# One pair of token tiles goes from a full to a seven-product second layer, in a fused windowed attention and squared-ReLU layer kernel, with a new order of all engines

## The chip, the cores and the metric

The kernel runs on one core of a Trainium2 chip. The metric is device time in microseconds (us) of one execution, lower is better. The profile is of one execution; its "span" runs from the first to the last instruction of the program.

## What is computed

Attention with a sliding window of 128 and 4 sink keys over 4 batches, 8 heads, 768 positions and 64 channels; its output, heads side by side, is the input of two matrix products with a squared ReLU between them. Inputs and output are float32; the kernel computes in bfloat16 and accumulates in float32.

```python
scores = scale * q @ k.T                      # per batch and head
keep = (key < 4) | ((0 <= row - key) & (row - key < 128))
a = softmax(where(keep, scores, -1e9))
x = (a @ v).transpose(0, 2, 1, 3).reshape(3072, 512)
r = maximum(x @ w_in, 0.0)                    # w_in 512 x 2048
out = (r * r) @ w_out                         # w_out 2048 x 512
```

## The kernel before

**Tiles.** A batch has six token tiles of 128 rows, taken as three pairs, (b, 0) to (b, 2). Attention of a pair: scores on TensorE (`ps`, L540), exp on ScalarE (`expm`, L561), masks on VectorE or by two affine selects on GpSimd (L200), the sinks' share and the values on TensorE (`po`, L596 and L621), division on VectorE (`xn_sb`, L636 and L637), and a transpose to `xT`. Layer 1 (`pm`) writes the squares into `gT_sb`, 16 blocks of the hidden width by 768 tokens, one batch at a time. Layer 2 reads `gT_sb` and writes the output.

**The start.** q and k of batch 0 come by eight transfers on the queues of SyncE and ScalarE (`qr`, L316), are cast by any of three engines (`qs`), turned by TensorE against an identity matrix (`ident`, built by one affine select of GpSimd, L227) into a PSUM bank `pt`, and copied out to `qkT`. Everything else that is loaded goes through GpSimd's queue with a cast to bfloat16: values (L343), `w_in` (L283), q and k of later batches (L332) and `w_out` (L289). Each of these loads takes one of eight semaphores in turn, so a load waits until the load eight places ahead of it has landed.

**Layer 2, two ways.** `layer2` (L927) is the plain product: for both tiles of a pair 16 products each, 128 rows by 512 columns, 32 products in all, then two copies out of PSUM and a store. `layer2_fast` (L1037) is a Strassen-like scheme on the 2 x 2 blocks of (tile, half of the hidden width): seven products of half the columns, each in 8 matmuls of 256 columns, so 56 matmuls. Around them stand four sums of `gT_sb` blocks on VectorE (`sg`, L995, the second of which overwrites a block of `gT_sb`), two copies, two pair sums (L1062), a last quarter (L1078), a middle part (L1088) and a first quarter. It also needs four sums of halves of `w_out` (`wt`, L968, VectorE), which wait for all four `w_out` loads. `CLASSIC` lists the pairs that take the plain way.

**The order.** The kernel lists its steps as numbered operations with their needs; the string `ORDER` says in which order they are written, and on which engine each runs: `65g` is step 65 on GpSimd (p TensorE, v VectorE, a ScalarE, g GpSimd, s SyncE). Each engine works through its own steps strictly in that order, and a PSUM or SBUF buffer goes to the next step that takes one. `+n` puts n dummy matmuls ahead of a TensorE step (L174; L1222 for the first ones), which fill time in which TensorE would stand idle. At the `sinks` steps a `+1` means something else: it picks the form with 64 rows of the array in place of 128.

```python
o, e = self.ops[int(n[:-1])], {"p": "pe", "v": "dve", "a": "act", "g": "pool", "s": "sp"}[n[-1]]
self.dummies = int(dummies or 0)
o.run(e)
```

Of the kernel before, what the change touches and what calls it, by code (L numbers as in the profile page):

```python
# [15 lines left out]
ALU = mybir.AluOpType  # L16

ORDER = """
0v 5g 1v 9a 11a 2v 8s 10s 12s 13a 15a 55a 3g 896p+37 19g 20g 21g 22g 23g 56v 57p 58a 65a 66v 67p+20 59v 68a 79p 99p
69v 80p 101a 14s 61v 60g 62p 82a 71v 70g 72p+8 73a 64v 87p+2 74v 88p 81a 63v 108p 89a 90a 83p 85p 6g 76v 110a 91p  # L20
93p+6 77p 86v 24g 4g 25g 26g 84v 95p 16s 109p 18s 7s 75g 102g 121g 94v 27g 92v 97p+5 98v 28g 29g 30g 78a 96a 100p
105p+1 152p 31g 32g 33g 34g 111v 112a 113v 103a 114p 104v 115p 116v 153a 154a 106p 107v 158p 159v 117p 119p 35g 120a
36g 164p 118v 155p 156v 157a 165v 161p 162a 173p 17s 122p 124a 174v 125p 127a 123v 37g 38g 126a 167p 39g 40g 175a
204v 168v 163v 131p 134a 140p 143a 170p 41g 135g 128p 129a 130p 132a 133g 42g 139p 171v 289p 166v 290p 169v 136p 291p
292p 137p 144v 172a 293p 141a 145p 142v 146p 138v 294p 295p 147v 148p 150p 160v 296p 151v 149a 179p 43g 44g 45g 274v
176p 275v 297v 180a 298a 46g 200p 202v 192p 188p 177a 194v 201p 193p 195v 203a 189p 191v 47g 190a 196p 276v 197p 199v
215p 216a 178v 198a 205v 48g 185p 218a 186v 234p 182p 49g 50g 51g 52g 206p 235a 53g 54g 355g 356g 219v 373s 357g 277v
358g 237a 238g 226p 207a 229a 299s 227a 181v 278p 279p 280p 208p 281p 183v 184v 209a 249p 211a 246p 247a 236v 282p
248v 359g 254p 251v 187a 374s 250v 252p 210v 283p 257a 300v 301v 253a 255a 256g 360g 376s 284p 302v 262p 265a 239p+1
240p 217v 303v 285p 375s 361g 241v 377s 212v 304p 220p 221v 263a 286a 287a 305p 307p 306v 308p 396p 397a 399a 230v  # L30
228g 231p+1 232p 362g 378s 363g 364g 365g 366g 379s 311p 309v 213p 233v 242p 244p 310v 214v 367g 312p 243a 245a 222p
380s 368g 313v 314v 258g 385g 381s 382s 224p 225a 369g 223a 315p 316v 370g 383s 389p 390a 392a 322p 398v 331p 323a
384s 371g 372g 400v 401p 391v 324a 317a 402v 596g 318s 332v 597g 259p 260p 393v 266g 264v 319p 320a 325p 321a 326a
394p 261v 395v 334p 335a 413p 598g 616s 615s 414a 415g 416a 267p+1 268p 599g 328p 386v 327v 333v 270p 271a 269v 336a
626v 617s 329a 330v 272p 337p 614s 338a 339v 273a 340p 341a 417g 600g 601g 342v 441v 460v 405p 406a 408a 343p 404s
344v 443v 352p 403s 409g 464p 288s 353a 407g 423p 424a 425g 387p 388a 461v 602g 465p 603g 604g 605g 467p 469a 619s
354v 462v 618s 620s 466a 442v 349p 468p 426a 470v 350a 427v 431p 432a 434a 463v 498v 410p+1 433g 345a 411p 412v 471p
472p 630p 633a 631a 621s 418p+1 419p 473v 475p 351a 500v 474v 476v 632v 428p 429p 420v 430v 346p 445p 499v 501v 503a
504v 446p 436p 448p 507v 435g 444v 437p 477a 347a 348v 447a 438v 451v 522p 523p 449p 524a 525v 526p 440s 506v 505v
452p 450a 478s 453p 527v 454v 528p 646p 647a 529p 479v 480v 649a 455v 456p 457v 483p 484p 458v 627v 481v 654p 502v  # L40
485a 657a 486p 487p 508p 509p 488a 655a 634v 635p 489v 482v 656g 490p 510a 530a 421s 439s 422s 536v 512p 636v 606g
607g 511v 532p 533p 514p 513v 515p 516a 491p 537v 582p 538v 518p 492v 493v 534v 535a 584v 494p 495v 496a 497s 608g
622s 519p 520v 609g 610g 568p 570a 583p 569p 540p 517a 542a 586p 572p 554p 571v 585v 555p 587v 573v 588p 589p 556a
557v 539v 521a 574p 575p 558p 560p 559v 611g 459s 541p 531a 625s 682v 543v 544p 545v 561p 576a 648g 578p 579p 580v
650g 590a 562a 563a 624s 546p 547p 548a 683v 564p 565p 566v 577a 592p 593p 594v 550p 551p 658g 686p 552v 549a 637p
638a 612g 687p 640a 684v 639v 641v 623s 628p 629a 689p 664p 595a 659p+1 660p 688v 567v 690p 613g 665a 642p 685v 553v
667a 668g 666g 691a 693p 692v 694p 643v 661v 591a 695v 581a 720v 696v 721v 722v 723v 672p 675a 676v 651p+1 652p 653v
697p 724p 726a 725p 727p 644s 730v 673a 674v 645s 728p 731p 677p 678p 739a 740v 698v 729a 662s 663s 699a 700s 669p
679v 701v 670p 744p 745p 746a 671v 681s 743v 742v 732p 705p 758p 747v 702v 759p 735p 748p 760a 706p 708p 707a 680s
749v 741v 761v 762p 764p 703v 704v 750p 751p 763v 733v 752a 773v 734v 736v 711v 710v 774v 772v 709p 712p 737a 714v  # L50
715v 754p 765p 766a 767a 755p 756v 713p 775v 804p 806a 805p 807v 768p 769p 770v 716p 790p 791p 717v 792a 718a 753a
808p 809v 776p 777p 778v 793v 771v 818p 819p 820a 757a 821v 810p 822p 794p 811p 780p 824p 823v 825p 812a 826a 779v
782p 781v 814p 783p 828p 738s 784a 796p 832v 795v 797p 798a 834v 835v 833v 813a 829p 830v 815p 816v 786p 787p 800p
801p 802v 831a 788v 836p 837p 839p 841v 719s 838a 840p 842v 799a 843p 827v 803a 817a 844p 785v 847p 789a 845v 870v
874p 851v 852v 855p 856p 871v 858p 875p 846v 848v 872v 849a 850s 857a 873v 853v 854v 860v 877p 876a 859p 861v 862p
864v 865v 863p 866p 867v 868v 869s 878p 880v 881p 882p 879v 883v 884g 887v 885p 890s 889a 888v 892a 886p 891s 893s
894v 895a
"""


# [47 lines left out]
def kernel(  # L108
# [188 lines left out]


    NATURAL, TURNED, BIASED, FAST = (2, 3), (), 1, (2, 3)
    CLASSIC = ((0, 0), (0, 1))  # L300
    GROUPS = {b: [(0, 6)] for b in range(B)}
    GROUPS[0] = [(0, 4), (512, 2)]
    if 1 not in NATURAL:
# [877 lines left out]
    for b in range(B):  # L1181
# [29 lines left out]
        for u in range(NS):  # L1211
            if (b, u) in CLASSIC:
                layer2(b, u, by_part=True)
# [46 lines left out]
```

## Time and profile before

| | |
|---|---|
| three timed runs | 207.95, 208.26 and 208.32 us, median 208.26 |
| the profiled execution | 207.93 us, of which the span is 206.2 us |
| TensorE matmul | busy 200.5 us, 97% of the span, granted clock 0.999 |
| VectorE, ScalarE, GpSimd | busy 172.3, 127.7 and 102.8 us |
| transfers | 26.09 MB, of which 12.59 MB through GpSimd's queue |

In the profile's rows PE is TensorE's matmul stream and PEld its weight loads, DVE is VectorE, ACT ScalarE, POOL GpSimd, SP SyncE; a q behind the name means the engine's sequencer, which issues transfers. A row of the timeline has start, length, engine, source line, operation, output<-inputs, shapes, and how many instructions were merged. In the chain of waits a row has start, length and what the span's end hung on at that time. Matmuls overlap, so a matmul's own length (273 ns for 256 columns) is not its pace: the pace is the distance of starts, which the pieces of the chain give.

### The profile page before, as it was taken

Reading aid. Unit: us, or ns where it says so; the run is one execution under the profiler, and the core shown is the slowest. Engines: PE = TensorE matmul, PEld = TensorE weight load, DVE = VectorE, ACT = ScalarE, POOL = GpSimd, SP = SyncE. Lnnn points to the kernel's source line nnn. Section 1 sums busy time; section 2 is a strip of 40 time slices with the busy share of each in tenths; the row PEclk is TensorE's granted clock in tenths of the full one; section 3 lists DMA queues with packets and bytes.
Section 4 is the critical chain, followed back from the end, with each engine's and each line's share of the span. In section 5 each row is a group of like instructions: output and inputs, shape, how many; then the busy total and the mean of one; then the engine's idle time right before and its main releaser. Section 6 shows DMA issues by size and latency. Waiting matters only on the chain.

```text
span 206.2 us, 5651 instructions
## 1 busy us (share of the span) xinstructions
PE 200.5 (97%) x2362; PEld 168.5 (82%) x2366; DVE 172.3 (84%) x307; ACT 127.7 (62%) x167; POOL 102.8 (50%) x141
## 2 busy tenths in 40 slices
PE   7999999999999999999999999999999999999993
PEld 7659996588557856668889889998889999998983
DVE  5688478778969767969989998999898799999953
ACT  3696188138787585797794364798964146787100
POOL 7899866898908999767960009920220000000001
PEclk9999999999999999999999999999999999999999
DMA  5999999999996999999993448999024311200205
GB/s 192 278 188 206 170 202 214 165 153 149 137 208 53 109 110 172 168 182 137 109 173 78 139 69 52 210 191 63 3 52 120 88 55 50 106 0 0 105 0 203
DMA packets 93881, 26.09 MB, mean 126 GB/s; under 512 B 86816, under 2 KB 91552, under 8 KB 93856
## 3 DMA queue, kind: packets, MB, share of 16 engines
q0 software_dynamic: 69248, 12.59, 86.0%
q1 hardware_dynamic: 23232, 11.90, 26.0%
q10 hardware_dynamic: 1376, 1.25, 1.8%
q8 instruction: 18, 0.29, 0.6%
q14 instruction: 7, 0.06, 0.1%
HBM read 27.30 MB, written 6.29 MB: 163 GB/s over the span
## 4 chain that ended last, share of the span: by engine, by line
PE 85%; ACT 6%; DVE 4%; issue 2%; POOLq 0%; ACTq 0%; DVEq 0%
PE py L1037 25%; PE pm L838 18%; PE pm L698 17%; PE py L927 7%; PE po L621 5%; PE ps L540 4%; ACT expm L561 3%; PE warm L1222 2%; PE pt L438 2%; ACT r L709 1%; PE po L596 1%; PE px L666 1%; PE pt L428 1%; DVE sg L995 1%; PE pt L174 1%
## 5 line engine op out<-in xcount | busy, mean ns | idle before, releaser
L200 POOL TENSOR_SCALAR_AFFINE_SELECT expm<-expm 128x512 bf16<-128x512 bf16 x42 | 31.3, 782 | 41.3 <-ACT expm L561 41.1
L561 ACT ACTIVATE expm<-ps 128x1024 bf16<-128x1024 f32 (+1 forms) x48 | 43.7, 954 | 9.4 <-PE ps L540 8.7
L698 PE MATMUL pm<-xT,w_in_sb 128*128 128x256 bf16 (+1 forms) x320 | 44.5, 294 | 0.2 <-ACT expm L561 0.2
L698 PEld LDWEIGHTS <-w_in_sb 128*128 128x128 bf16 x320 | 34.3, 114 | 6.8 <-issue 0.9
L1037 PEld LDWEIGHTS <-gT_sb 128*128 128x128 bf16 x336 | 30.7, 98 | 4.2 <-issue 0.5
L1078 POOL TENSOR_TENSOR osb<-osb,u 128x256 f32<-128x256 f32 x1 | 0.7, 727 | 51.1 <-DVE u L1062 51.1
L1037 PEld LDWEIGHTS <-sg 128*128 128x128 bf16 x240 | 23.0, 98 | 2.7
L838 PE MATMUL pm<-xs,w_in_sb 128*128 128x128 bf16 (+1 forms) x256 | 23.4, 246 | 0.0
L838 PEld LDWEIGHTS <-w_in_sb 128*128 128x128 bf16 x256 | 21.9, 114 | 0.2 <-issue 0.2
L343 POOL DMA_DIRECT2D v<-in_v_dram x24 | 21.5, 905 | 0.1
L1037 PE MATMUL py<-wt,gT_sb 128*128 128x256 bf16 x160 | 20.8, 273 | 0.2 <-DVE gT_sb L995 0.2
L1037 PE MATMUL py<-wt,sg 128*128 128x256 bf16 x160 | 20.6, 273 | 0.0
L860 ACT ACTIVATE gT_sb<-r 128x1024 bf16<-128x1024 bf16 x19 | 19.4, 1053 | 1.5 <-DVE r L906 1.5
L709 ACT ACTIVATE r<-pm 128x1024 bf16<-128x1024 f32 x14 | 14.2, 1022 | 8.9 <-PE pm L698 8.9
L332 POOL DMA_DIRECT2D qn<-in_k_dram x20 | 17.8, 899 | 2.1 <-DMA v<-in_v_dram 1.0
L1037 PE MATMUL py<-w_out_sb,gT_sb 128*128 128x256 bf16 x144 | 18.7, 273 | 0.0
L332 POOL DMA_DIRECT2D qn<-in_q_dram x20 | 17.7, 894 | 1.8 <-DMA w_out_sb<-in_moe_w_out_dram 1.4
L879 DVE TENSOR_TENSOR t<-t,pm 128x512 f32<-128x512 f32 x24 | 16.0, 682 | 2.5 <-PE pm L838 2.0
L637 DVE TENSOR_TENSOR xn_sb<-po,rc 128x512 bf16<-128x512 f32 (+1 forms) x26 | 16.9, 650 | 0.9
L894 ACT ACTIVATE r<-pm 128x1024 bf16<-128x1024 f32 x12 | 12.1, 1020 | 8.8 <-PE pm L838 8.7
L838 PEld LDWEIGHTS <-qkT 128*128 128x128 bf16 x192 | 16.6, 114 | 0.1
L711 DVE TENSOR_SCALAR r<-pm 128x1024 bf16<-128x1024 f32 x10 | 12.1, 1220 | 4.6 <-PE pm L698 4.5
(99 smaller groups left out, 348.4 us busy)
## 6 DMA issues: line engine op xcount, KB each, us to landing
out_dram<-osb SPq DMA_DIRECT2D x11, 512.0 KB, 3.5
v<-in_v_dram POOLq DMA_DIRECT2D x24, 128.0 KB, 6.8
qn<-in_k_dram POOLq DMA_DIRECT2D x20, 128.0 KB, 6.5
qn<-in_q_dram POOLq DMA_DIRECT2D x20, 128.0 KB, 6.5
w_in_sb<-in_moe_w_in_dram POOLq DMA_DIRECT2D x4, 512.0 KB, 9.0
w_out_sb<-in_moe_w_out_dram POOLq DMA_DIRECT2D x4, 512.0 KB, 11.0
qr<-in_q_dram ACTq DMA_DIRECT2D x4, 256.0 KB, 6.6
qr<-in_k_dram SPq DMA_DIRECT2D x4, 256.0 KB, 6.2
```

The costliest lines, as they stand in the source:

```text
L200: nc.gpsimd.affine_select(out=e_tile, in_=e_tile, compare_op=ALU.is_ge, fill=fill, base=i - 1, pattern=[[0, n], [1 if i else -1, 128]], ch ...
L332: nc.gpsimd.dma_start(out=qn_t[b, ti][:, t, :].rearrange("p (h d) -> p h d", d=D), in_=(q, k)[ti][b, :, 128 * t:128 * t + 128, :].rearrang ...
L343: nc.gpsimd.dma_start(out=v_sb[b % 2][:, t, :, 0:D], in_=v[b, :, 128 * t:128 * t + 128, :].rearrange("h p d -> p h d"))
L561: nc.scalar.activation(out=x[:, :, o:512], in_=bank_t["s", b, s, m][:, :, o:512], func=AF.Exp, scale=scale)
L637: touch(("po", b, s, m0), e, nc.vector.tensor_tensor(out=xn_sb[:, 2 * s:2 * s + 2, :].rearrange("p i (j q h d) -> q p j i h d", j=2, q=2, ...
L698: nc.tensor.matmul(pm[:, i, :], lhsT=w_in_sb[:, fb // 4, kb, fb % 4:512:4], rhs=xT[:, c0 // 256:(c0 + cw) // 256, kb, :], start=(kb == 0), ...
L709: nc.scalar.activation(out=o, in_=h, func=AF.Relu)
L838: touch(tag, e, nc.tensor.matmul(y[:, bk, i, :], lhsT=weights(name, f0 + i, a), rhs=rhs[:, a, :], start=fresh and i == 0 and a == 0, stop= ...
L860: nc.scalar.activation(out=d, in_=x, func=AF.Square)
L879: touch(tag, e, nc.vector.tensor_tensor(out=T["t"], in0=T["t"], in1=T["y"][:, bk], op=ALU.subtract), bk)
L927: touch((b, u), e, nc.tensor.matmul(pm[:, i, :], lhsT=gT_sb[:, fb, 128 * t:128 * t + 128], rhs=w_out_sb[:, fb, :], start=(fb == 0), stop=( ...
L1037: ins = nc.tensor.matmul(y_, lhsT=x[:, i, :], rhs=r_, start=(first or tail and n == 2) and i == 0, stop=i == HB - 1, skip_group_check=not ...
```

## The change

Pair (0, 0), the first two token tiles of batch 0, leaves `CLASSIC`: its second layer is written by `layer2_fast`. Pair (0, 1) keeps the plain way, and all other pairs have the fast one already. Steps 278 to 288 become 278 to 296, and all later numbers rise by 8. The whole `ORDER` is another one, with another choice of engine at many steps and other counts of dummies; the rest of the program is the same.

```diff
-0v 5g 1v 9a 11a 2v 8s 10s 12s 13a 15a 55a 3g 896p+37 19g 20g 21g 22g 23g 56v 57p 58a 65a 66v 67p+20 59v 68a 79p 99p
+9a 11a 0v 1v 5g 8s 10s 12s 14s 13a 4g 15a 904p+43 19g 20g 3g 65g 21g 55v 56v 57p 58v 59a 60a 99p+13 101a 22g 66v 67p
...
-    CLASSIC = ((0, 0), (0, 1))
+    CLASSIC = ((0, 1),)
```

Counted over the order strings: the dummies are 37 + 20 + 8 + 2 + 6 + 5 before and 43 + 13 + 11 + 3 + 6 + 2 after, 78 both times. The sinks steps in the 64-row form are 8 of 16 before and 9 after; one more of them stands ahead of the first layer-1 step. VectorE has 7 in place of 10 relu steps of layer 1 and second-half quads, ScalarE 29 in place of 26; masks on GpSimd are 23 in place of 21.

Three places of the order matter below. The first is GpSimd at the start of the program, before the change, from the bias table of the scores (`biases`) on:

```order
L200 AFFINE_SELECT biases<-biases 128x2x128 x2
L237 COPY biases<-biases 128x512
L238 MEMSET biases 4x256
L227 AFFINE_SELECT ident<-ident 128x128
L343 DMA v_181<-in_v_dram 128x8x64 x2
L283 DMA w_in_sb<-in_moe_w_in_dram 128x4x512
L343 DMA v_181<-in_v_dram 128x8x64 x2
L184 CAST qs<-qr 128x512 x2
```

And the same place now:

```order
L200 AFFINE_SELECT biases<-biases 128x2x128 x2
L237 COPY biases<-biases 128x512
L238 MEMSET biases 4x256
L200 AFFINE_SELECT tri<-tri 128x128 x2
L343 DMA v_181<-in_v_dram 128x8x64 x2
L227 AFFINE_SELECT ident<-ident 128x128
L184 CAST qs<-qr 128x512
L283 DMA w_in_sb<-in_moe_w_in_dram 128x4x512
L343 DMA v_181<-in_v_dram 128x8x64 x2
L283 DMA w_in_sb<-in_moe_w_in_dram 128x4x512
L184 CAST qs<-qr 128x512
```

The identity matrix has moved behind the mask triangles (`tri`) and two loads of values, and the second cast behind two `w_in` loads.

The second is GpSimd in the middle, where it goes from loads for batches 1 and 2 to the masks of batch 1 (`expm`). Before:

```order
L343 DMA v_182<-in_v_dram 128x8x64 x2
L332 DMA qn<-in_k_dram 128x8x64 x2
L332 DMA qn<-in_q_dram 128x8x64 x2
L200 AFFINE_SELECT expm<-expm 128x4x128 x2
L343 DMA v_181<-in_v_dram 128x8x64
L200 AFFINE_SELECT expm<-expm 128x4x128 x2
```

And now, where `mask_168` is the mask table that batches from 1 on need for their first pair, which GpSimd built at 16 us before:

```order
L343 DMA v_182<-in_v_dram 128x8x64 x2
L332 DMA qn<-in_k_dram 128x8x64 x2
L332 DMA qn<-in_q_dram 128x8x64 x2
L343 DMA v_181<-in_v_dram 128x8x64 x2
L241 COPY mask_168<-tri 128x128
L242 COPY mask_168<-tri 128x256
L243 MEMSET mask_168 4x256
L200 AFFINE_SELECT expm<-expm 128x4x128 x8
```

Two loads of values and the table now stand ahead of four masks (two selects each) in one block.

The third is SyncE's queue at the end, with the stores of the last pair, before:

```order
L1120 DMA out_dram<-osb 128x1024
L1120 DMA out_dram<-osb 128x2x512
L1127 DMA out_dram<-osb 128x256 x2
L1135 DMA out_dram<-osb 128x128
L1255 UNCONDITIONAL_BRANCH
```

And now:

```order
L1120 DMA out_dram<-osb 128x1024
L1120 DMA out_dram<-osb 128x2x512
L1131 DMA out_dram<-osb 128x256
L1127 DMA out_dram<-osb 128x256
L1135 DMA out_dram<-osb 128x128 x2
L1255 UNCONDITIONAL_BRANCH
```

SyncE has four stores of the last pair in place of three, both halves of the last quarter (L1135) among them; ScalarE's queue has one in place of two.

More of the change, by code (lines that the diff above doesn't have):

```diff
@@ L18 @@
 ORDER = """
-0v 5g 1v 9a 11a 2v 8s 10s 12s 13a 15a 55a 3g 896p+37 19g 20g 21g 22g 23g 56v 57p 58a 65a 66v 67p+20 59v 68a 79p 99p
[L20 to L57, printed above, removed]
+9a 11a 0v 1v 5g 8s 10s 12s 14s 13a 4g 15a 904p+43 19g 20g 3g 65g 21g 55v 56v 57p 58v 59a 60a 99p+13 101a 22g 66v 67p
+61v 69v 62p+11 63a 23g 24g 64a 70g 71v 79p 81a 102v 16s 80p 68v 72p+3 73v 87p 74a 88p 83p 25g 26g 82a 76v 84v 108p 85p
@@ new lines @@
+89a 91p 90a 86v 93p+6 110a 77p 78a 109p 95p 92v 94v 97p+2 100p 7s 6g 75g 112a 111g 105p+1 114p+1 96v 98v 152p 113v
+115p 27g 28g 29g 30g 31g 103a 104v 106p 158p 116v 107v 117p 119p 32g 33g 34g 153a 154v 164p 118v 165v 159a 35g 36g
+120a 155p 156a 161p 162a 2v 204g 173p 122p 123a 125p 127v 126v 163a 124a 174v 167p 168v 37g 38g 139p 166a 141a 131p
+134a 39g 40g 41g 135g 42g 170p 43g 128p 129a 44g 45g 46g 47g 48g 49g 50g 51g 52g 53g 130p 157v 142v 132a 133v 54g 363g
+364g 140p 143a 365g 366g 297p 298p 144v 136p 145p 137p 138v 146p 147v 175a 169a 274v 275v 276v 277v 160a 171a 172a
@@ new lines @@
+299p 300p 278v 301p 302p 381s 279v 280v 148p 149a 367g 368g 303p 150p 151a 304p 305a 306a 307s 179p 180a 176p 177a
+200p 202v 192p 194a 193p 195v 201p 196p 203v 197p 199a 198v 178v 121g 188p 189p 190a 215p 185p 191v 205v 218a 216a
+234p 235a 237a 236g 238g 186v 281v 182p 206p 207a 181v 183a 226p 187v 282p 284v 283p 285p 184v 308v 383s 227a 208p
+288v 229a 211a 230g 228g 287v 369g 246p 209a 370g 371g 372g 373g 310v 384s 309v 286p 289p 249p 251a 247a 250a 210v
+291v 290p 248v 293p 374g 375g 376g 377g 219v 252p 254p 253a 292v 294v 382s 295v 255a 257a 217v 312p 314a 313p 212v
@@ new lines @@
+258g 262p 263a 256g 265a 231p+1 311v 315p 318v 232p 233v 213p 214v 316p 220p 266g 385s 319p 404p 221v 317v 388s 407a
+405a 239p+1 240p 241v 320p 222p 224p 225a 223a 242p 244p 243v 321v 245v 323p 397p 386s 398a 322v 324v 325a 342p 264g
+406v 400a 401v 333p 334a 17s 339p 343v 387s 390s 378g 379g 380g 408v 604g 18s 392s 340a 259p 260p 261v 389s 391s 399v
+330p 605g 623s 409p 410v 402p 403v 606g 607g 344v 331a 345p 346a 421p 422a 423g 424a 267p+1 335v 268p 341v 634v 348p
+336p 394v 347a 349a 350a 270p 269v 272p 332v 326s 271v 273v 425g 327p 328a 337v 338a 329v 622s 468v 469v 470v 625s
@@ new lines @@
+360p 413p 416a 361v 449v 471v 393g 351p 624s 352a 472p 473p 431p 608g 609g 450v 414a 415v 434a 432a 395p 475p 396a
+477v 474v 478v 451v 357p 358a 417g 476p 610g 611g 635v 612g 411s 412s 439p 506v 442a 418p+1 440a 419p 420v 479p 480p
+433v 638p 362a 296s 639a 641a 627s 613g 508v 626s 629s 481v 628s 353v 482v 426p+1 427p 428v 483p 435g 484v 485a 486s
+436p 453p 454p 430s 456p 437p 507v 438v 511a 512v 354p 640v 443g 359v 444p 452v 441g 445p 530p 531p 455a 457p 460p
+458a 532a 534p 446v 448s 459v 533v 429s 642v 513v 447s 355a 356a 462v 514v 461p 536p 654p 657a 655a 535v 464p 487v
@@ new lines @@
+537p 463v 488v 491p 492p 515v 465v 466a 467s 538a 662p 509v 489v 540p 490v 510v 493a 494p 663a 664g 665a 643p 495p
+614g 615g 644v 497v 544v 616g 617g 618g 539a 496a 516p 518a 517p 541p 546v 520p 519v 542v 498p 499p 656g 619g 547v
+576p 578a 521v 577p 522p 523p 590p 502p 620g 621g 579v 500v 501v 545v 524a 525a 526p 527p 580p 592a 591p 582p 594p
+631s 503v 504a 528v 543a 562p 564a 563p 581v 583p 630s 566p 548p 529a 593v 596p 595v 597p 658g 632s 565v 567v 690v
+666g 505s 691v 584a 550a 568p 569p 570a 549p 552p 586p 692v 587p 551v 553v 572p 588v 598a 554p 573p 585a 574v 555p
@@ new lines @@
+599a 556a 600p 601p 602v 694p 558p 559p 560v 561v 557a 645p 646a 696a 647v 648a 695p 649v 693v 633s 636p 637a 697p
+672p 675a 676g 571v 603v 700v 667p+1 668p 669v 698p 673a 650p 701p 651v 699a 703v 702p 674g 653s 652s 575a 589a 728v
+729v 680p 681a 730v 731v 659p+1 660p 704v 705p 706v 732p 683a 734a 682v 747a 707a 733p 735p 737a 684g 709v 749v 748v
+661v 670s 708s 736p 677p 678p 679v 739p 752p 753p 754a 755v 685p 710v 686p 766p 738v 756p 767p 768a 770p 687v 740p
+689s 743p 713p 769v 688s 771v 750v 714p 757v 758p 759p 760a 751v 741v 742v 744v 745a 711v 712v 716p 718a 715a 772p
@@ new lines @@
+773p 774a 775a 762p 763p 717p 671s 780v 720p 781v 719v 784p 785p 761a 764v 786a 787v 776p 777p 778v 765a 722v 723v
+721p 724p 788p 782v 789v 812p 814a 725v 726a 798p 800a 813p 816p 815v 817v 799p 826p 828a 779a 827p 818p 802p 819p
+820a 821a 801v 804p 829v 803v 840v 830p 832p 805p 790p 791p 783v 822p 823p 841v 806a 842v 808p 831v 833p 792a 794p
+824v 809p 810v 844p 845p 843v 746s 795p 796v 727s 834a 793a 836p 837p 838v 807a 847p 835a 849v 846a 848p 825a 850v
+851p 797a 852p 855p 811v 839a 859v 853v 863p 860v 854v 865a 861v 878v 864p 866p 856v 857a 862v 880v 867p 870p 868a
@@ L58 @@
+858s 879v 882p 883p 872v 869v 873v 871p 884v 888v 874p 875v 876a 885p 887a 886p 881v 889p 877s 891v 892v 897s 890p
+893p 894p 895v 896v 898a 899s 900v 901s 902a 903s
 """
```

## The prediction

> **What bounds the kernel now.** I read the busy shares first, then the slices, the chain that ended last, and last the chain's pieces in order of time.
>
> ```profile
> PE 200.5 (97%) x2362; PEld 168.5 (82%) x2366; DVE 172.3 (84%) x307; ACT 127.7 (62%) x167; POOL 102.8 (50%) x141
> PE   7999999999999999999999999999999999999993
> PE 85%; ACT 6%; DVE 4%; issue 2%; POOLq 0%; ACTq 0%; DVEq 0%
> 16.15 1.91 PE pm L698 x16
> ```
>
> TensorE is busy 97% of the span, and only its first and last slices are below 9 tenths. 85% of the chain is TensorE. The last row is the first piece of layer 1, at 16.15 us: from there TensorE has work without a hole until its last product, so the time is the **start** (16.15), the **sum of TensorE's pieces**, and the **tail** behind its last product. VectorE, at 84%, is the nearest rival.
>
> **Times.** The sum is made against the profiled execution, 207.93 us (span 206.2 and 1.7 around it). The median of the three runs is 208.26, 0.33 above it. I work out a difference and apply it to the median.
>
> **The products.** A piece gives the pace: its length over its count.
>
> ```profile
> 36.33 1.73 PE py L927 x8
> 65.74 2.62 PE py L1037 x24
> 18.06 0.23 PE po L596 x4
> 62.94 0.11 PE po L596 x4
> ```
>
> A full product takes 1.73 / 8 = 0.216 us, a half one 2.62 / 24 = 0.109. Pair (0, 0) had 32 full ones, 32 x 0.216 = 6.91 us; it gets 56 half ones, 56 x 0.109 = 6.11: **-0.80 us**. The third row is a sinks step in the 128-row form behind the first layer-1 step, the fourth one in the 64-row form. One such 0.23 step leaves the stream and stands now ahead of layer 1, where TensorE waits for others: **-0.23**. The dummies (78) and the number of changes between 64 and 128 rows behind the first layer-1 step (I count 40 in both orders) stay.
>
> **VectorE under it.** The fast pair adds four sums, two copies, two pair sums, two middle parts and two quarters; the plain copies go.
>
> ```profile
> 193.81 0.69 DVE L995 TENSOR_TENSOR sg<-gT_sb,sg 128x1024 bf16<-128x1024 bf16 x1
> 201.21 0.42 DVE L1062 TENSOR_TENSOR u<-py,u 128x256 f32<-128x256 f32 x1
> 40.00:50.00 10.00, 9.95 (x106) 8.31 (x104) 7.75 (x14) 5.31 (x9) 9.05 (x12) 1.00 2.68 152
> 50.00:60.00 10.00, 9.95 (x102) 6.23 (x103) 8.51 (x15) 7.62 (x11) 6.23 (x7) 1.00 2.44 163
> L711 DVE TENSOR_SCALAR r<-pm 128x1024 bf16<-128x1024 f32 x10 | 12.1, 1220 | 4.6 <-PE pm L698 4.5
> ```
>
> Four sums at 0.69 and some six small steps at 0.42 are 2.8 + 2.5 = 5.3 us. The windows (after the length: PE, PEld, DVE, ACT, POOL) show VectorE 7.75 and 8.51 busy of 10 where this lies, so 3.7 us are free there, and the three relus that leave VectorE (1.22 each, last row) free 3.7 more. I cost it at nothing, hidden by TensorE's stream; with the cover gone it would be 5.3 - 3.7 = 1.6 us. What is late next then are the masks and squares that VectorE makes for the same stretch.
>
> **The start.** GpSimd now makes the identity matrix behind the triangles and two loads.
>
> ```profile
> 3.33 0.28 POOL L227 TENSOR_SCALAR_AFFINE_SELECT ident<-ident 128x128 bf16<-128x128 bf16 x1
> 3.57 1.96 POOL L343 DMA_DIRECT2D v<-in_v_dram  x2
> 5.00 0.41 PE L428 MATMUL pt<-ident,qs 64*128 64x64 bf16 x16
> 5.47 0.60 ACT L181 ACTIVATE qkT<-pt 128x512 bf16<-128x512 bf16 x1 [0.53 <-PE pt L428]
> 8.72 0.58 PE L428 MATMUL pt<-ident,qs 64*128 64x64 bf16 x16
> 9.83 0.57 PE L428 MATMUL pt<-ident,qs 64*128 64x64 bf16 x16
> 10.96 3.13 ACT L561 ACTIVATE expm<-ps 128x768 bf16<-128x768 f32 x4
> 11.08 0.55 POOL L200 TENSOR_SCALAR_AFFINE_SELECT tri<-tri 128x128 bf16<-128x128 bf16 x2
> 15.05 1.94 ACT L561 ACTIVATE expm<-ps 128x1024 bf16<-128x1024 f32 x2
> 16.15 1.04 PE L698 MATMUL pm<-xT,w_in_sb 128*128 128x256 bf16 x8 [0.17 <-ACT expm L561]
> ```
>
> The identity was ready at 3.61. Now: 3.37 (end of the bias table) + 0.55 + 1.96 + 0.28, **6.1 to 6.2**, so the first transposes go from 5.00 to about 6.1. Behind them I went on by hand with the new order and these durations: copies out of the bank at 6.6, the casts that follow them, second transposes at 7.8, third at 8.9 (8.72 before: they wait for late q anyway), fourth at about 10.95 (9.83 before), and the exps begin at 11.9 instead of 10.96. A copy of 0.60 that ScalarE made between its exps (`xT`) is VectorE's now, so the exp that frees the bank for the last step ahead of layer 1 ends at 16.3, not 16.1. Behind it still stands a sinks step of 0.11 with its change of rows, so layer 1 begins at about 16.55: **+0.40**. The ends: +1.1, if the whole delay of the identity passes through, and -0.6, if nothing of it does and the copy's 0.60 is won. The value lies by the row it is nearest to, that of the exps.
>
> **The tail.**
>
> ```profile
> 201.67 0.80 DVE L1094 TENSOR_TENSOR osb<-py,u 128x256 f32<-128x256 f32 x2
> 201.84 1.06 PE L1037 MATMUL ya<-w_out_sb,gT_sb 128*128 128x128 bf16 x16
> 202.12 0.82 SPq L1127 DMA_DIRECT2D out_dram<-osb  x2
> 202.93 0.29 DVE L183 COPY osb<-ya 128x128 f32<-128x128 f32 x1 [0.47 <-PE ya L1037]
> 203.31 0.33 SPq L1135 DMA_DIRECT2D out_dram<-osb  x1
> ```
>
> The last store was issued at 203.31, 0.57 behind TensorE's end (202.74: 16 products of 0.056 from 201.84). Two stores of SyncE took 0.82, and now three stand in a row behind VectorE's last parts, with one of ScalarE's moved over; I reckon the last issue 0.8 behind TensorE's end: **+0.22**. The ends are 0 and +0.66 (two issues of 0.33, none hidden).
>
> **Sum**: -0.80 - 0.23 + 0.40 + 0.22 = -0.41, so 207.5 for a profiled execution and **207.9 us** as the median.
>
> **A rule against it.** In this trace a product of half the columns costs half (0.216, 0.109). The Trainium skill ("TensorE: Matmul & The Clock Gate", section "Back-to-back issue gap") says that in a stream of weight loads and products the pace is set by both, some 81 ns at 128 columns and 131 at 512. By a straight line between them I estimate 98 ns at 256, and 56 x 98 - 32 x 131 = +1.3 us in place of -0.80, a time of about 210.0. The rows quoted disagree with its 131.
>
> **Rivals.** *The start and the tail cost nothing*: -1.03, **207.2**. For it: the third transposes wait for late q in both orders. Against: the first two do not.
>
> *The whole delay passes*: -1.03 + 1.1 at the start + 0.3 at the tail = +0.4, **208.6**. For it: the chain through start has no spare time that I can see between transposes and exps. Against: the copy that left ScalarE.
>
> *Products paced by weight loads.*
>
> ```profile
> L698 PEld LDWEIGHTS <-w_in_sb 128*128 128x128 bf16 x320 | 34.3, 114 | 6.8 <-issue 0.9
> L1037 PEld LDWEIGHTS <-gT_sb 128*128 128x128 bf16 x336 | 30.7, 98 | 4.2 <-issue 0.5
> ```
>
> Loads took 98 and 114 ns, about as long as a half product. Were each of the 56 held to 114, they would take 6.4 us and save 0.5: **208.1**. Against: the 24 products at 0.109.
>
> *GpSimd's masks come late*, the rival on the other side. Its rows of before:
>
> ```profile
> 16.14 0.74 POOL L241 COPY mask<-tri 128x128 bf16<-128x128 bf16 x1
> 16.83 0.86 POOL L242 COPY mask<-tri 128x256 bf16<-128x256 bf16 x1
> 33.02 1.23 POOL L200 TENSOR_SCALAR_AFFINE_SELECT expm<-expm 128x512 bf16<-128x512 bf16 x2
> 46.94 0.87 POOL L332 DMA_DIRECT2D qn<-in_q_dram  x1 [0.37 <-issue]
> 53.31 2.07 POOL L200 TENSOR_SCALAR_AFFINE_SELECT expm<-expm 128x512 bf16<-128x512 bf16 x2
> 65.38 0.36 PE po L621 x12
> qn<-in_q_dram POOLq DMA_DIRECT2D x20, 128.0 KB, 6.5
> w_in_sb<-in_moe_w_in_dram POOLq DMA_DIRECT2D x4, 512.0 KB, 9.0
> ```
>
> The second of the two moved value loads waits for the load eight places ahead, the one of 46.94. With a landing of 6.5 us that is 53.4; then 0.9 for the issue, 1.9 for the table (0.74 + 0.86 + its memset's 0.3) and four masks of 1.23 to 2.07: the last is ready at 61.1 to 64.5. TensorE wants it for values at about 65.5. So it is hidden while a mask takes under (65.5 - 56.2) / 4 = 2.3 us; with a landing of 9.0, as the larger loads have, and the dear masks it is 67.0, a stall of 1.5 us, and 207.9 + 1.5 = **209.4**. Behind that waiting load on GpSimd stand the masks and the next q and k loads of batch 2, and TensorE waits for both.
>
> *New waits elsewhere*: over half of VectorE's steps stand at another place in the new order, and before had almost no holes left. A hole of 0.8 us or more in the stretch behind 75 us, which I have not followed step by step, makes 208.7 or more.
>
> **How the numbers follow.** Chances: forecast 0.40 (own range 207.5 to 208.3), start and tail free 0.20, whole delay 0.12, weight loads 0.03, late masks 0.15, new waits elsewhere 0.10. A measurement of this kernel can tell about 0.2%, 0.42 us, from no change. Faster by more: half of the forecast and the free start, 0.40. Within: the other half, the weight loads and 0.05 of the whole delay, 0.28. Slower: the rest, 0.32. The low end goes below 207.2 for the copy won on ScalarE, to 206.9; the high end takes in the late masks, 209.4. What lies outside are dearer stalls and, on the low side, the -0.6 in full.
>
> **What would show it.** First transposes at 6.1, exps from 11.9, the first layer-1 product at 16.55; pair (0, 0) in pieces of eight at 0.87, seven of them; TensorE's last product some 0.6 earlier than 202.74; the last store 0.8 behind it. GpSimd's four masks done before the values at 65. Wrong: a hole on TensorE behind 17 us of more than 0.3, VectorE the releaser of it, or pieces of eight longer than 0.87.

## The result, and the profile after

The changed kernel takes **207.64 us** (median of 12 runs) and the kernel before 208.09 (median of 12, measured beside it): a ratio of 0.9976, with a 95% interval of 0.9967 to 0.9984. That is 0.45 us less by the medians, and 0.33 to 0.69 by the interval. One of the twelve runs took 212.03 us and is left out of the ratio. The profiled execution took 207.74 us, span 206.0; the one before 207.93, span 206.2. So the two profiles differ by 0.2 us and the medians by 0.45, and what the profiles show of single terms is uncertain by about that difference.

From the page of the changed kernel, the same three lines as before the change:

```profile
PE 200.9 (97%) x2390; PEld 171.7 (83%) x2390; DVE 168.1 (82%) x304; ACT 131.6 (64%) x174; POOL 106.6 (52%) x148
PE   7999999999999999999999999999999999999993
PE 90%; DVE 4%; POOL 2%; issue 1%; ACT 1%; DVEq 0%; POOLq 0%; ACTq 0%
```

TensorE is still the bound. VectorE has 4 us less to do, ScalarE and GpSimd 4 us more each.

The start, in order of time (start, length, engine, line, operation):

```profile
5.87 0.30 POOL L227 TENSOR_SCALAR_AFFINE_SELECT ident<-ident 128x128 bf16<-128x128 bf16 x1
6.23 0.61 PE L428 MATMUL pt<-ident,qs 64*128 64x64 bf16 x16 [0.33 <-POOL ident L227]
8.97 0.41 PE L428 MATMUL pt<-ident,qs 64*128 64x64 bf16 x16
10.99 0.41 PE L428 MATMUL pt<-ident,qs 64*128 64x64 bf16 x16
11.92 3.13 ACT L561 ACTIVATE expm<-ps 128x768 bf16<-128x768 f32 x4
16.52 1.72 PE L698 MATMUL pm<-xT,w_in_sb 128*128 128x256 bf16 x14
```

The first transposes wait for the identity matrix and come 1.23 us later (6.23 against 5.00). The third come 0.25 later, the fourth 1.16, the exps 0.96, and layer 1 begins 0.37 later.

Of the pieces in the chain of waits, one of the new products, and the two places where the chain leaves TensorE for short:

```profile
57.83 1.75 PE py L1037 x16
87.81 0.70 DVE xn_sb L637
88.56 0.40 PE px L666 x4
124.15 0.50 ACT t L181
124.69 0.61 PE pm L838 x8
```

Sixteen half products in 1.75 us are 0.109 each. In the second and third row TensorE's transposes of `xn_sb` start only when VectorE's division is done (87.81 + 0.70), and in the last two its quad products start when ScalarE has copied the bank. TensorE stood for 0.30 us at the first place and 0.27 at the second, by the distance of its starts against their usual distance. It has three more waits of about 0.1 each (at 62, 143 and 175, 0.28 together). The kernel before has two holes behind 60 us, 0.23 at 97 and 0.26 at 151, 0.49 together, and both are gone.

The tail:

```profile
201.56 1.06 PE L1037 MATMUL ya<-w_out_sb,gT_sb 128*128 128x128 bf16 x16
202.53 0.34 SPq L1127 DMA_DIRECT2D out_dram<-osb  x1
202.70 0.28 ACT L181 ACTIVATE osb<-ya 128x128 f32<-128x128 f32 x1 [3.07 <-DVE osb L183]
202.97 0.89 SPq L1135 DMA_DIRECT2D out_dram<-osb  x2
```

TensorE ends at 201.56 + 16 x 0.056 = 202.46. The data of the last store is ready at 202.98, but SyncE issues two stores in a row (0.89 for both) and is done at 203.86.

So the profiled difference of -0.2 us is +0.37 at the start, -0.65 in the stream (202.46 - 16.52 = 185.94 against 202.74 - 16.15 = 186.59), and +0.07 from TensorE's end to the span's end (3.49 us before, 3.56 now).

### The profile page after: what moved, and what is told of

Read it like the earlier page. It is cut to its first block, busy times and chain, and to the rows that moved or that the text cites. A ratio compares the mean times of both kernels' runs of the same rounds, so it can differ in the third digit from the quotient of the medians.

```text
span 206.0 us, 5703 instructions
## 1 busy us (share of the span) xinstructions
PE 200.9 (97%) x2390; PEld 171.7 (83%) x2390; DVE 168.1 (82%) x304; ACT 131.6 (64%) x174; POOL 106.6 (52%) x148
## 4 chain that ended last, share of the span: by engine, by line
PE 90%; DVE 4%; POOL 2%; issue 1%; ACT 1%; DVEq 0%; POOLq 0%; ACTq 0%
PE py L1037 31%; PE pm L698 18%; PE pm L838 17%; PE ps L540 6%; PE po L621 5%; PE py L927 3%; PE pt L438 2%; PE px L666 1%; PE po L596 1%; DVE xn_sb L637 1%; POOL v L343 1%; DVE gT_sb L720 1%; PE ps L533 1%; PE pk L501 1%; PE pt L428 1%
## 5 line engine op out<-in xcount | busy, mean ns | idle before, releaser
L200 POOL TENSOR_SCALAR_AFFINE_SELECT expm<-expm 128x512 bf16<-128x512 bf16 x46 | 35.1, 808 | 39.7 <-ACT expm L561 37.5
L1037 PEld LDWEIGHTS <-gT_sb 128*128 128x128 bf16 x368 | 33.9, 98 | 4.4 <-issue 0.8
L709 ACT ACTIVATE r<-pm 128x1024 bf16<-128x1024 f32 x17 | 17.4, 1024 | 16.3 <-PE pm L698 16.3
L1037 PEld LDWEIGHTS <-sg 128*128 128x128 bf16 x264 | 25.0, 98 | 2.9 <-issue 0.3
L1037 PE MATMUL py<-wt,sg 128*128 128x256 bf16 x176 | 22.8, 272 | 0.0
L1037 PE MATMUL py<-wt,gT_sb 128*128 128x256 bf16 x176 | 22.7, 273 | 0.0
L1037 PE MATMUL py<-w_out_sb,gT_sb 128*128 128x256 bf16 x160 | 20.8, 273 | 0.0
L860 ACT ACTIVATE gT_sb<-r 128x1024 bf16<-128x1024 bf16 x20 | 20.4, 1055 | 0.1
L894 ACT ACTIVATE r<-pm 128x1024 bf16<-128x1024 f32 x12 | 12.1, 1024 | 7.0 <-PE pm L838 6.9
L181 ACT ACTIVATE osb<-py 128x256 f32<-128x256 f32 (+1 forms) x19 | 7.6, 408 | 13.3 <-DVE osb L1088 10.4
L906 DVE CUSTOM_DVE_ANT_1 r<-pm,t 128x1024 bf16<-128x1024 f32 x12 | 14.5, 1222 | 1.8 <-PE pm L838 1.4
```

Source lines behind the costliest of these rows:

```text
L200: nc.gpsimd.affine_select(out=e_tile, in_=e_tile, compare_op=ALU.is_ge, fill=fill, base=i - 1, pattern=[[0, n], [1 if i else -1, 128]], ch ...
L709: nc.scalar.activation(out=o, in_=h, func=AF.Relu)
L860: nc.scalar.activation(out=d, in_=x, func=AF.Square)
L906: touch(tag, e, nc.vector._custom_dve(TENSOR_ADD_SAT, out=r.rearrange("p b n c -> p b (n c)"), in0=T["y"].rearrange("p b n c -> p b (n c)" ...
L1037: ins = nc.tensor.matmul(y_, lhsT=x[:, i, :], rhs=r_, start=(first or tail and n == 2) and i == 0, stop=i == HB - 1, skip_group_check=not ...
```

## The experiments

Each kernel is the changed one with an edit of the order, unless it says otherwise, and was timed beside the kernel before. Medians are compared with the changed kernel's 207.64, ratios are to the kernel before.

**What the products give.** `x4_plain` takes pair (0, 0) the plain way again inside the new order: eight steps of layer 2 at the places of the seven products, two copies (one of ScalarE, one of VectorE), no sums.

```diff
-    CLASSIC = ((0, 1),)
+    CLASSIC = ((0, 0), (0, 1))
-278v 279v 280v ... 281v ... 282p 284v 283p 285p ... 288v ... 287v ... 286p 289p ... 291v 290p 293p ... 292v 294v ... 295v ... 296s
+278p 279p 280p ... 281p 282p ... 283p 284p 285p ... 286a ... 287v ... 288s
```

> The changed order with pair (0, 0) taken the plain way again: 32 products of 512 columns in place of 56 of 256, two copies, no sums on VectorE for it; all else as in the changed kernel. Theory (the products give 0.80 us and nothing else comes of them): 207.64 + 0.80 = 208.44, with TensorE's stream from 16.52 longer by 0.8. Rival (VectorE's extra 5.3 us for the fast pair cost part of it back as holes): the plain version is slower by 0.4 us or less, at most 208.05.

It took 208.43 us, ratio 1.0019 (1.0008 to 1.003): 0.79 us slower than the changed kernel, where 0.80 was expected. The medians are uncertain by some 0.2, so the hundredth is luck, but the two profiles say the same: summed over the distances of TensorE's starts, the products of layer 2 take 0.79 us more. So VectorE's extra sums cost nothing that can be seen. It also says that the new order with the plain pair is 0.34 us slower than the old order (0.17 to 0.62 by the interval): the gain is that of the products, less what the rest of the new order costs.

**Where the order gives it back: two holes.** `x3_holes` closes both, `z1_hole88` only the first (its first two lines).

```diff
-341v 634v 348p 336p 394v 347a 349a 350a 270p 269v 272p
+341v 269v 634v 348p 336p 394v 347a 349a 350a 270p 272p
-539a 496a 516p 518a 517p
+539a 516p 518a 496a 517p
```

> Two places of the order are changed. VectorE divides the last values of batch 1 ahead of the sink values of batch 3 and the sink keys of batch 2 (TensorE waited 0.30 us at 88.56 for this division), and ScalarE copies the first quad sum ahead of the copy for the layer-2 scheme (TensorE waited 0.27 us at 124.69 for the bank). Theory (the stream's missing 0.37 us lies in these two holes): both holes go and the time falls by 0.4 to 0.57 us, to 207.1 to 207.25. Rival (what waits there is late elsewhere next, or the holes are shared slack): one or both holes come back within 15 us and the time falls by less than 0.2 us.

> Only one of the two holes is closed: VectorE divides the last values of batch 1 ahead of the sink values of batch 3 and the sink keys of batch 2. Theory (each hole counts by its own length): -0.30 us of the changed kernel's 207.64, to 207.25 to 207.4, with the hole of 0.27 at 124 us still there. Rival (one of the two made the whole gain of 0.64): 207.0, or no gain at all.

`x3_holes` took 207.00 us, ratio 0.995 (0.9937 to 0.9962), 0.64 less than the changed kernel; `z1_hole88` took 207.17, ratio 0.996 (0.9947 to 0.9974), 0.47 less. The theory holds for the sum, whose 0.64 is a little more than the 0.57 of both holes. The first place was worth more than its 0.30 and the second less than 0.27, but the intervals are 0.25 us to either side, so the split stays open. The pieces of the chain in `y1_both`, which has both edits, show no step of another engine at either place:

```profile
84.52 3.47 PE pm L698 x16
87.99 0.45 PE px L666 x8
88.44 3.47 PE pm L698 x24
121.85 0.87 PE py L1037 x8
122.72 1.79 PE pm L838 x32
124.51 1.75 PE py L1037 x16
```

**The tail.** `x1_tail` gives the last store to ScalarE, which makes its data; `y1_both` has this and both closed holes.

```diff
-902a 903s
+902a 903a
```

> Only the last store moves: the second half of the last quarter (128x128) is issued by ScalarE, which makes it, in place of SyncE behind the first half. In the changed kernel this store was issued at 203.46 us, 0.48 behind its data (202.98), since SyncE issued the first half until 203.37. Theory (SyncE's row of stores sets the end): the last issue goes to about 203.0 and the time falls by 0.3 to 0.45 us, to about 207.3. Rival (the end hangs on the landing of the other stores, or ScalarE's queue lands later): less than 0.1 us, 207.55 to 207.75.

> The two edits that closed the holes at 88 and 124 us and the store of the last half on ScalarE's queue, together. Theory (a hole in TensorE's stream and the tail are separate terms of the sum): the gains add, 207.64 - 0.64 - 0.23 = 206.77 us. Rival (the end hangs on how the last stores land, and an earlier end meets the same queue): less than 0.1 us below 207.00.

`x1_tail` took 207.41 us, ratio 0.9969 (0.9958 to 0.998): 0.23 less, between the theory (0.3 to 0.45) and the rival (under 0.1), and nearer the theory. `y1_both` took 206.70, ratio 0.9934 (0.9917 to 0.9951): the gains add (206.77 expected). Its last stores:

```profile
201.81 0.28 ACT L181 ACTIVATE osb<-ya 128x128 f32<-128x128 f32 x1 [3.07 <-DVE osb L183]
202.08 0.40 SPq L1135 DMA_DIRECT2D out_dram<-osb  x1
202.12 0.37 ACTq L1135 DMA_DIRECT2D out_dram<-osb  x1
out_dram<-osb SPq DMA_DIRECT2D x1, 64.0 KB, 1.7
out_dram<-osb ACTq DMA_DIRECT2D x1, 64.0 KB, 1.9
```

The two halves are now issued side by side, 0.03 behind the data (201.81 + 0.28). The last issue is done 0.40 us behind its data, where it was 0.88 (203.86 - 202.98); of these 0.48, 0.2 go to a landing of 1.9 us in place of 1.7 (last rows: us from issue to landing), and what remains fits the 0.23.

**The start.** Three runs. `x2_ident` makes the identity first in the new order, `y4_late_ident` makes it late in the order of before, and `z4_sinks` puts the second sinks step back behind the first layer-1 step. The dummies follow, so that they do not stand in the way.

```diff
-14s 13a 4g 15a 904p+43 19g 20g 3g 65g
+14s 13a 3g 4g 15a 904p+37 19g 20g 65g
```

```diff
-55a 3g 896p+37 19g 20g 21g
+55a 896p+43 19g 20g 3g 21g
```

```diff
-105p+1 114p+1 96v 98v 152p 113v
+105p+1 96v 98v 152p 114p 113v
```

> The identity matrix is made ahead of the triangles and the two value loads, and the first dummies are 37 in place of 43 so that they do not stand ahead of the first transposes. Theory (the start is late because of the identity): first transposes at about 5.1 to 5.3 in place of 6.23, first layer-1 product up to 0.37 us earlier (16.15 to 16.3 in place of 16.52), time 207.3 to 207.5. Rival (the exps on ScalarE and the arrival of q and k set the start): the first transposes move, layer 1 begins at 16.4 to 16.55 and the time stays within 0.1 us of 207.64.

> The kernel before with the identity matrix built behind the first two value loads (ready at 3.37 + 1.96 + 0.28 = 5.6 in place of 3.61) and 43 first dummies in place of 37; first transposes at 5.7 in place of 5.00. Theory (in the order of before the start is swallowed by late q and k: third transposes wait for q in any case): time within 0.2 us of 208.1. Rival (the whole delay passes through): slower by 0.6 to 0.7 us, 208.7 to 208.8.

> The second sinks step of pair (0, 1) goes back behind the first layer-1 step, in the form with 128 rows, as it stood in the kernel before. Theory of the prediction (it costs 0.23 us in the stream, and ahead of layer 1 it costs what the start waits for): the first layer-1 product comes 0.2 to 0.3 us earlier, since the step waited 0.20 for its bank and took 0.11, the stream is 0.23 longer, and the time is within 0.15 us of 207.64. Rival (the start is set by other things, and the step was free there): slower by 0.2 to 0.25 us, 207.85 to 207.9.

`x2_ident` took 207.53 us, 0.11 less. In its profile:

```profile
5.40 0.62 PE L428 MATMUL pt<-ident,qs 64*128 64x64 bf16 x16 [0.55 <-DVE qs L183]
9.53 0.29 PE L428 MATMUL pt<-ident,qs 64*128 64x64 bf16 x8 [1.12 <-DVE qs L183]
16.96 1.28 PE L698 MATMUL pm<-xT,w_in_sb 128*128 128x256 bf16 x10
```

The first transposes come 0.83 earlier than in the changed kernel, but half of the third ones then stand 1.12 us for a cast that waits for q, and layer 1 begins later than in the changed kernel's profile. That execution took 208.2 us, one of the longest of twelve (207.46 to 208.2): how late q lands differs from run to run, and where it is late, q counts and not the identity. The time lies between the theory's range (207.3 to 207.5) and the rival's, and the profile shows the rival's mechanism. `y4_late_ident` took 208.26, ratio 1.0009 (0.9998 to 1.0019), with first transposes at 5.68 and layer 1 at 16.38: of 0.68 us of delay about 0.2 arrive, and by the interval it may be none. Both say that the identity's delay is mostly swallowed on its way to layer 1. `z4_sinks` took 207.56, 0.08 less, with the first layer-1 product at 16.09:

```profile
15.87 0.28 PE L596 MATMUL po<-vs,es 64*128 64x130 bf16 x4
16.09 1.93 PE L698 MATMUL pm<-xT,w_in_sb 128*128 128x256 bf16 x16
```

So the sinks step ahead of layer 1 kept TensorE about as long (its bank, 0.20, and its own 0.11) as it would have taken in the stream (0.23). Single executions differ here: nine profiles with the start of the changed kernel have layer 1 at 16.31 to 17.00, the middle one at 16.47, and only the 16.09 of `z4_sinks` lies clearly outside. Moving it gave nothing, as the theory said of the sum of both.

**GpSimd's masks.** `y2_masks2` puts two loads ahead of the block of four masks, `y3_masks5` five (369g to 373g), and `z2_split` the two loads between the masks. The diffs are those of the first and the last.

```diff
-236g 238g ... 230g 228g 369g ... 370g
+369g 370g 236g 238g ... 230g 228g
```

```diff
-236g 238g ... 230g 228g 369g ... 370g
+236g 369g 238g 370g ... 230g 228g
```

> Two loads of q and k of batch 2 (0.9 us each on GpSimd) stand ahead of the block of four masks. In the changed kernel the last of the masks ended at 62.74 and the values that need it began at 65.94, so 3.2 us are spare. Theory (late masks cost only beyond that slack): the last mask ends at 64.5, no wait, time 207.55 to 207.75. Rival (the masks were already what TensorE waits for there, or the moved loads wait for landings): slower by 0.5 us or more.

> Five loads (four of q and k, one of values; 4.4 us on GpSimd) stand ahead of the four masks. Theory: the last mask ends at 62.74 + 4.4 = 67.1, TensorE waits at the values of batch 1 for 67.1 - 65.94 = 1.2 us, and the time is 208.6 to 209.0. Rival (other work of TensorE, VectorE or ScalarE behind the wait had slack, and the hole is shared): slower by less than 0.5 us.

> The same two loads of q and k as in the run with two loads ahead of the masks (211.24 us), but put between the masks: first mask, load, second mask, load, third and fourth. In that run one sum of VectorE (0.69 us elsewhere) stood from 57.34 to 61.96, while eight selects of GpSimd ran without a break from 57.26 to 62.45, and TensorE waited 2.79 us for a copy queued behind that sum. Theory (a VectorE step that meets the start of an unbroken row of selects is held for most of the row; issuing a load breaks the row): no VectorE step over 2 us there, time 207.5 to 208.3. Rival (the loads themselves are what is too early, or GpSimd is simply late): 210 us or more.

`y2_masks2` took 211.24 us, ratio 1.0152 (1.0124 to 1.0181), and `y3_masks5` 209.71, ratio 1.0075 (1.0049 to 1.0101). Two loads cost 3.6 us, more than five (2.1). Neither the theory of slack nor that of late masks says that: with five loads the last select still ended at 65.58, ahead of the values' 65.94. In the changed kernel the masks were not what TensorE waited for. GpSimd and VectorE there, and the values that read the masks:

```profile
55.72 7.03 POOL L200 TENSOR_SCALAR_AFFINE_SELECT expm<-expm 128x512 bf16<-128x512 bf16 x8
57.78 1.04 DVE L995 TENSOR_TENSOR sg<-sg,gT_sb 128x1024 bf16<-128x1024 bf16 x1
65.94 1.01 PE L621 MATMUL po<-v,expm 128*128 128x65 bf16 x28
```

The same place with two loads ahead:

```profile
57.26 5.19 POOL L200 TENSOR_SCALAR_AFFINE_SELECT expm<-expm 128x512 bf16<-128x512 bf16 x8
57.34 4.62 DVE L995 TENSOR_TENSOR sg<-sg,gT_sb 128x1024 bf16<-128x1024 bf16 x1
63.72 0.41 DVE L183 COPY qkT<-pt 128x512 bf16<-128x512 bf16 x1
64.18 0.29 PE L501 MATMUL pk<-qkT,kblk 128*32 128x256 bf16 x4 [2.63 <-DVE qkT L183]
```

And with five:

```profile
60.28 4.04 DVE L570 TENSOR_TENSOR expm<-expm,mask 128x768 bf16<-128x768 bf16 x1
60.31 5.27 POOL L200 TENSOR_SCALAR_AFFINE_SELECT expm<-expm 128x512 bf16<-128x512 bf16 x8
```

In both a step of VectorE that starts within 0.1 us of GpSimd's row of selects (a sum of 0.69 us in the first, a mask product of 0.55 in the second) lasts until six or seven of the eight selects are done, 4.62 and 4.04 us, and a copy queued behind it makes TensorE wait. The row of selects is fast there: 5.2 / 8 = 0.65 us each. In the changed kernel the two engines met half-way through each other's steps and took turns: selects of 0.88, sums of 1.04, nobody held. The Trainium skill ("SBUF — State Buffer", section "SBUF: two separate sides") says that VectorE and GpSimd share a pair of ports by an exclusive lock, and that a VectorE step with two inputs in SBUF waits while a GpSimd instruction that began first has it. The rows agree with the lock, but not with its length: the page has it held for one instruction, and here it is held over five or six selects in a row. Nor does who began first decide it in the second case, where VectorE's record begins 0.03 us ahead of the selects (starts on GpSimd are rough).

`z2_split` took 207.63 us, ratio 0.9987 (0.9972 to 1.0002), with the same two loads. Its longest VectorE step there:

```profile
57.57 0.90 POOL L332 DMA_DIRECT2D qn<-in_k_dram  x1
57.71 1.13 DVE L995 TENSOR_TENSOR sg<-sg,gT_sb 128x1024 bf16<-128x1024 bf16 x1
```

So the loads themselves were not the cause, and neither were late masks: the 3.6 us came from how the row of selects met VectorE. What removed the hold is not shown: the loads now break the row, but its first select also stands where it stands in the changed kernel (55.68 and 55.72), which has no hold in its profile either, and one of the twelve runs took 209.18 us.

The same hold comes with no edit of the masks. The profiled executions of `x1_tail` (210.94 us), `x3_holes` (209.97) and `z1_hole88` (211.42) have the changed kernel's order at this place. That of `x1_tail`:

```profile
55.95 5.30 DVE L720 TENSOR_TENSOR gT_sb<-r 128x1024 bf16<-128x1024 bf16 x1
55.97 4.73 POOL L200 TENSOR_SCALAR_AFFINE_SELECT expm<-expm 128x512 bf16<-128x512 bf16 x8
62.70 1.03 PE L1037 MATMUL py<-wt,gT_sb 128*128 128x256 bf16 x8 [2.19 <-DVE u L183]
```

In all three a square of VectorE (0.68 us elsewhere) that begins 0.02 to 0.18 us ahead of the row lasts 5.30 to 5.46 us, past the row's end, and TensorE stands for 2.4 to 2.5 us. So the changed order itself runs into the hold in some executions; its run of 212.03 us has no profile. The kernel before, whose masks here stand in rows of two selects, took at most 208.78 us in all its runs.

**All of it together.** `z3_all` has the closed holes, the store and the early identity.

> Both holes closed, the last half's store on ScalarE, and the identity matrix first with 37 dummies. Theory (start, stream and tail are separate terms): 206.70 - 0.1 = 206.6 us, the first layer-1 product at 16.4 to 16.5. Rival (the earlier transposes meet late q, as one run of the early identity did, and what they gain is lost to waiting): 206.65 to 206.9.

It took 206.64 us, ratio 0.9931 (0.9914 to 0.9949), with layer 1 at 16.28. It is faster than both kernels; from `y1_both` (206.70) it can't be told apart, as the run of the early identity alone suggested.

## Why the prediction was right, point by point

- **The products**: -0.80 predicted, 0.79 measured by undoing the pair alone (`x4_plain`). Pieces of eight take 0.87. This mechanism was right.
- **The sinks step**: -0.23 in the stream is right, but it was not a gain of its own. What the stream gave, the start took (`z4_sinks`, 0.08 between the two places). The prediction had the second half of this inside its +0.40.
- **The start**: +0.40 predicted, +0.37 in the profile, with the times on the way as worked out (transposes at 6.23 for 6.1 to 6.2, exps at 11.92 for 11.9, layer 1 at 16.52 for 16.55). That one execution met it to 0.03 is luck, with 16.31 to 17.00 in nine. The words on the cause were too simple, too: the identity itself accounts for 0.1 to 0.2 of it at most (`x2_ident`, `y4_late_ident`), and the sinks step in front of layer 1 for most of the rest.
- **The tail**: +0.22 predicted. The issue of the last store was done 1.40 us behind TensorE's end (203.86 - 202.46) in place of 0.90 (203.64 - 202.74), 0.5 more and not 0.22. From TensorE's end to the span's end the two profiles differ by 0.07 only, but the one before is a single execution: `y4_late_ident`, which has the old tail, shows 3.33 us in place of 3.49, while nine profiles with the changed tail show 3.55 to 3.57 and the three with the store moved to ScalarE 3.31 to 3.36. So the changed tail cost 0.07 to 0.23 us, and `x1_tail` got 0.23 back: the term was of about the right size.
- **The step that failed** is "I cost it at nothing, hidden by TensorE's stream", for VectorE. It holds for the sums of the new pair (`x4_plain`), and not for the new order of VectorE's and ScalarE's other steps: the stream got 0.65 shorter in place of 1.03. The waits that came are 0.85 us together (two holes of 0.57, three short ones of 0.28), the holes that went 0.49, and the difference of 0.36 is nearly all that is missing. The two large ones lay behind 75 us, in the stretch that was priced only as a rival ("a hole of 0.8 us or more"), and closing them gave 0.64 (`x3_holes`). VectorE's division releases the first of them, of 0.30 us, so the prediction's own sign of being wrong (a hole of more than 0.3 with VectorE the releaser) is just reached and not passed; and TensorE's last product came 0.28 earlier, not some 0.6.
- **The total**: -0.41 forecast, -0.45 measured. By the two profiles the sum is -0.2 and not -0.41, as the stream is short by 0.38 and the tail came out at +0.07 there. The agreement of the medians to 0.04 is therefore partly luck.
- **The rival of the late masks** had the right place and the wrong mechanism. There were 3.2 us to spare (the last mask at 62.74, the values at 65.94), so neither dear masks nor a landing at 9 us alone would have reached TensorE. What does reach it is VectorE held by the selects, which cost 3.6 us for a shift of 1.8 us on GpSimd, and came with no shift at all in three profiles.
- **Products paced by weight loads**, and the rule that the prediction quotes against itself: the products of 256 columns ran at 109 ns in the new pair too, and undoing it cost 0.79, so both are ruled out here.

## What to carry to other kernels

When the bound is one engine's unbroken stream, the price of a change of algorithm is its instructions times their pace, and that part came out here as reckoned (0.80 and 0.79); what a new order does to the other engines decides whether it arrives. After such a change, look in the chain of waits for the few short pieces that leave the bound engine: here three small edits of the order were worth twice the change itself. And when two engines get in each other's way, ask how their steps meet before worrying about how late a row ends, and look at single executions too: the same order can meet the hold in one and miss it in the next. To break a long row of the one with something that uses neither is worth a try; the one run that did so (`z2_split`) does not prove it.

## What the runs showed of the hardware that was not expected

VectorE and GpSimd at SBUF: a sum of 0.69 us took 1.04 when it met a running row of selects half-way, and 4.62 when it started 0.08 us after the row. A square of 0.68 took 5.30 when it started 0.02 us ahead of the row.

A hole of 2.8 us on TensorE costs more than its length. In `y2_masks2` the windows after the hole (length, then PE, PEld, DVE, ACT, POOL, the granted clock, DMA share) are

```profile
64.00:65.00 1.00, 0.82 (x16) 0.53 (x17) 1.00 (x4) 0.40 (x2) 1.00 (x2) 1.00 0.19 9
65.00:66.40 1.40, 1.38 (x10) 1.07 (x9) 1.40 (x4) 1.40 (x2) 1.40 (x3) 0.60 1.53 222
66.40:68.20 1.80, 1.80 (x10) 1.11 (x8) 0.99 (x2) 0.73 (x2) 1.80 (x3) 0.50 2.16 172
```

and eight half products, which span 1.04 us elsewhere, span

```profile
66.50 1.91 PE L1037 MATMUL py<-wt,gT_sb 128*128 128x256 bf16 x8
```

About one us after work resumes the clock falls to half, for 3 to 3.5 us. Three of its six runs had a mean clock of 0.989 to 0.992 and took 211.8 to 212.1 us, three had 1.000 and took 210.5 to 210.7. If their holes are as long as the profiled one, which is of the first group, the second group is the hole alone (207.64 + 2.8 = 210.4), and the first pays some 1.4 us more. With five loads the hole was 1.8 us and the clock stayed at 1.00. Between these it goes either way: behind a hole of 2.5 us the clock fell in the profile of `z1_hole88` (mean 0.990), and behind one of 2.4 in that of `x3_holes` it did not (1.000). The Trainium skill ("TensorE: Matmul & The Clock Gate", section "What's actually happening") puts the fall to half rate after an idle window of about 3.4 us; here 2.8 us were enough in the profiled run, and by the mean clock in half of the six.
